# At the end of layer 1: the last pair's sum product ahead of its value products, and its transposes ahead of the preceding pair's output product

## The chip, the cores and the metric

The kernel runs on one core of one Trainium2 chip. The metric is the device time of one execution in microseconds (us); lower is better. Where two kernels are compared, the ratio is the mean time of one kernel's fast runs over that of the other's fast runs of the same rounds, so it is not quite the ratio of the medians that are quoted beside it. Intervals are 95%.

## The reference, cut to what matters

Two identical layers are applied to one token of 640 numbers. Each is an attention over a key and value cache (32 heads of 192, the last 4096 positions) and a gated MLP, each with a layer norm ahead and a residual after it:

```python
    x = A_x
    x = x + _A_ref(_layernorm(x, axis=-1), A_k_cache, A_v_cache, A_wq, A_wo)
    x = x + _B_ref(_layernorm(x, axis=-1), B_w_gate, B_w_up, B_w_down)
    x = x + _A_ref(_layernorm(x, axis=-1), A_k_cache, A_v_cache, A_wq, A_wo)
    x = x + _B_ref(_layernorm(x, axis=-1), B_w_gate, B_w_up, B_w_down)
```

With a single token every product is a matrix times a vector, so the kernel reads far more than it computes: 218 MB of keys, values and weights in some 514 us.

## The kernel before

The heads are worked on in 16 pairs, 0 to 15. For each pair there is a query product `Q`, scores `QK`, a softmax, value products `PVmm` (scores times values, followed by a copy of the result by ScalarE), a sum product `RS` (the softmax's sum, spread to all partitions, and its reciprocal on VectorE), transposes `PVt` of the copied result (and the scaling by the reciprocal on VectorE), and an output product `PVn` with that pair's part of the output weights, which adds into `yT`. The helpers record operations, and each engine executes its own in the order of recording; `ex=[rb[i]]` makes an operation wait for the other engines' last use of PSUM bank i.

```python
        def RS(z, bk=4):
            so = 260 if bk == 2 else 2 * DH
            sm = bank[bk][:, so:so + 2]
            pg.op("pe", lambda t: t.matmul(sm, lhsT=ones_f, rhs=rs2[z], start=True, stop=True), rd=[res(f"rs2{z}"), res("ones")], wr=[res("rsum")], ex=[rb[bk]])
            for h in range(2):
                rb[bk].last["dve"] = pg.op("dve", lambda v, h=h: v.reciprocal(out=Rn[z][64 * h:64 * h + 64], in_=sm[64 * h:64 * h + 64, h:h + 1]),
                                          rd=[res("rsum")], wr=[res(f"Rn{z}{h}")])
        # ... PVmm: 32 matmuls into two banks and a ScalarE copy of each bank; in the last pair the
        #     values come in two loads, three quarters (b1) and one quarter (b0), and the products that
        #     need b0 are a part of their own (24 matmuls, then 8) ...
        def PVt(z, sums=True):
            if sums:
                RS(z)
            # ... tm: six small matmuls from o8_sb into oT3, which lies in bank 2 ...
            pg.op("pe", tm, rd=[res("o8sb0"), res("o8sb1"), res("cst")], ex=[rb[2]])
            pg.op("dve", lambda v: v.tensor_scalar(out=oTb[z], in0=oT3[:, 0:3], scalar1=Rn[z], scalar2=None, op0=ALU.mult),
                  rd=[res(f"Rn{z}0"), res(f"Rn{z}1")], wr=[res(f"oTb{z}")], ex=[rb[2]])
        # ... PVn: 15 matmuls of wo and oTb[z] into yT; for pairs 14 and 15 they wait for the load "wol" ...
        if l == 0:
            # ... pairs 0 to 14 ...
            p = NPAIR - 1
            PVmm(p, 1)
            RS(1, 2)
            PVn(p - 1, 0)
            PVt(1, False)
            PVn(p, 1)
```

Then come the residual and the MLP of the layer, which begins with a mean over all partitions (`ln_mean`, one float32 matmul), a centring on VectorE, and the gate products.

All loads go through one queue, in a fixed order. SyncE issues a load when its buffer has come free. Around the end of layer 1 the order is:

```python
    def last_values(l, p):
        return [("b1", l, p), ("b0", l, p)]
    seq = [("a", 0, 0)] + [("c", 0, p) for p in range(1, 15)] + [("a", 0, 15), ("b", 0, 14)] + last_values(0, 15)
    seq += [("wol", 14), ("wol", 15)] + [(k,) for k in (*MD, "v1", "wq2", "v0", "v2", "v3", "v4", "wq3", "wom")] + # ...
```

So the values of pair 15 (`b1`, then the last quarter `b0`) are followed by the output weights of pairs 14 and 15, then by the gate weights `wg0` and `wg2` and two pieces of up weights. Those eight are issued in one go, near 258 to 262 us. The next load, `d0` (480 KB of down weights), goes into cells that held the first gate weights, so it is issued only when the first group of gate products is done. That is the first transfer that has to wait for the code that the change touches.

Of the kernel before, what the change touches and what calls it, by code (L numbers as in the profile page):

```python
# [109 lines left out]
def decode_kernel(ctx: ExitStack, nc, cx: bass.AP, uc: bass.AP,  # L110
# [66 lines left out]
    def res(name):  # L177
        if name not in R:
            R[name] = _Res(name)
        return R[name]  # L180
# [13 lines left out]
    def slot(s, o, n):  # L194
        return big[:, PLACE[s] * UNIT + o:PLACE[s] * UNIT + o + n]

    def v_at(p):
        return 0 if p % 2 else WOE
# [12 lines left out]
    def mreg(o, n):  # L211
        return big[:, M0 + o:M0 + o + n]
# [165 lines left out]
    def ln_sq(xi):  # L378
        ln_center(xi, 1, xc, res("xc"))
        pg.op("dve", lambda v: v.tensor_tensor_reduce(out=sq, in0=xc, in1=xc, scale=1.0 / D, scalar=0.0, op0=ALU.mult, op1=ALU.add,  # L380
                                                      accum_out=ss_c), rd=[res("xc")], wr=[res("sq"), res("ss")], multi=True)

    def ln_rstd(k2, eps_ap, out_ap, rout):
        pg.op("pe", lambda t: t.matmul(dmx[:, 0:1], lhsT=ones_f, rhs=ss_c, start=True, stop=True), rd=[res("ss"), res("ones")], ex=[rb[2]])
        pg.op("act", lambda a: a.activation(out=lnv_c, in_=dmx[:, 0:1], func=ACT.Ln, bias=eps_ap, scale=k2), rd=[res("eps")], wr=[res("lnv")], ex=[rb[2]])
        pg.op("act", lambda a: a.activation(out=out_ap, in_=lnv_c, func=ACT.Exp, scale=-0.5), rd=[res("lnv")], wr=[rout])
# [7 lines left out]
    def attention(l, xi):  # L394
# [6 lines left out]
        def Q(p, y, bk=2):  # L401
            qe = bank[bk][:, 0:P]
            sa = A_SLOT[l][p]
            w, rw = slot(sa, 0, WQE), [rslot[sa]]
            if (l, p) == (1, 2):
                w, rw = mreg(0, WQE), rc[0:WQE // FW]
            elif (l, p) == (1, 3):
                s2 = A_SLOT[l][2]
                w, rw = slot(s2, 0, WQE), [rslot[s2], res("wq3")]

            def f(t):
                for i, c0 in enumerate((0, P, 2 * P)):
                    for c in range(DC):
                        ins = t.matmul(qe[:, i:i + 1], lhsT=w[:, c * 2 * DH + c0:c * 2 * DH + c0 + P], rhs=xq[:, c:c + 1], start=(c == 0), stop=(c == DC - 1))  # L414
                return ins
            ev = pg.op("pe", f, rd=[res("xq")] + rw, ex=[rb[bk]])
            if y is None:
                pg.op("dve", lambda v: v.tensor_copy(out=q2, in_=qe[:, 0:3]), wr=[res("q2")], ex=[rb[bk]])
                return ev
            pg.op("dve", lambda v: v.tensor_tensor(out=qs[:, y], in0=qe[:, 0:3].unsqueeze(2).to_broadcast([P, 3, 32]), in1=mask3, op=ALU.mult),  # L420
                  rd=[res("cst")], wr=[res(f"qs{y}")], ex=[rb[bk]])
            return ev
# [49 lines left out]
# [8 lines that stand above are left out]
        def PVmm(p, z):  # L480
            inm = l == 1 and p == PM
            sv = None if inm else B_SLOT[l][p]
            half = (l, p) in halves
            for h in (1, 0) if half else (0, 1):
                vt = (mreg(h * NB * DH, NB * DH) if inm else slot(sv, v_at(p) + h * NB * DH, NB * DH)).rearrange("p (t d) -> p t d", t=NB)
                for part in (1, 0) if half and h == 0 else (None,):
                    us = range(NB // 2) if part is None else range(part * NB // 4, (part + 1) * NB // 4)
                    first = range(NB // 4, NB // 4 + 4) if part is not None else range(4)
                    final = range(NB // 4 - 4, NB // 4) if part is not None else range(NB // 2 - 4, NB // 2)

                    def f(t, h=h, vt=vt, us=us, first=first, final=final):
                        for u in us:
                            j = u % 4
                            ins = t.matmul(o8[h][32 * j:32 * j + 2, 0:2 * DH].rearrange("p (a d) -> p a d", a=2), lhsT=et_sb[:, z, h * NB + 2 * u:h * NB + 2 * u + 2],  # L494
                                           rhs=vt[:, 2 * u:2 * u + 2, :], start=u in first, stop=u in final, tile_position=(0, 32 * j))
                        return ins
                    rV = rc if inm else [rslot[sv]] + ([res("bh0")] if part == 0 else []) if half else [rval[sv]]
                    ev = pg.op("pe", f, rd=[res(f"et{z}")] + rV, ex=[rb[4 + h]])
                    if not inm and not half:
                        rslot[sv].rd.append(ev)  # L500
                pg.op("act", lambda a, h=h: a.copy(out=o8_sb[:, :, h * DH:(h + 1) * DH], in_=o8[h][:, 0:2 * DH].rearrange("p (a d) -> p a d", a=2)),  # L501
                      wr=[res(f"o8sb{h}")], ex=[rb[4 + h]])
# [5 lines left out]
# [4 lines that stand above are left out]
            def tm(t):  # L512
                for c in range(3):
                    for sg in range(2):
                        ins = t.matmul(oT3[:, c:c + 1], lhsT=o8_sb[:, sg, c:2 * DH:3], rhs=mask2[:, sg:sg + 1], start=(sg == 0), stop=(sg == 1))
                return ins
# [3 lines that stand above are left out]
# [72 lines left out]
        if l == 0:  # L592
            Q(0, 0)
            ln_sq(xi)
            QK(0, 0)
            ln_rstd(K2_ATT, eps_a, srs_c, res("srs"))
            soft(0, scale_pm)
            expo()
            ET(0)
            step(1, 0)  # L600
            loop(1, 14)
            p = NPAIR - 1
            PVmm(p, 1)
            RS(1, 2)
            PVn(p - 1, 0)
            PVt(1, False)
            PVn(p, 1)
        else:
            mark("a14_0", Q(14, 0))
            mark("QM", Q(PM, 1, 5))  # L610
            def unstow(i):
                o, n = sum(m for _, m in stash[:i]), stash[i][1]
                pg.op("dve", lambda v: words(v, mreg(o, n), stash[i][0]), rd=[res(f"stash{i}")], wr=rc[o // FW:-(-(o + n) // FW)],
                      ex=[rb[SB[i][0]]], own="st")
            for i in (3, 4, 5):
                unstow(i)
            ln_sq(xi)
            mark("a14_1", QK(14, 0, ks=(0,)))
            mark("a14_2", QK(14, 0, ks=(1, 2)))
            Q(15, 0)  # L620
            ln_rstd(K2_ATT, eps_a, srs_c, res("srs"))
            QK(15, 0, 1)
            soft(0, scale_pm)
            expo()
            ET(0)
            Q(0, 0)
            soft(1, hook=lambda: (Q(2, None), QK(0, 0)))
            for i in (2, 0, 1):
                unstow(i)
            expo(1)  # L630
            soft(0, mid=lambda: PVmm(14, 0))
            PVout(14, 0)
            ET(1)
            expo()
            PVmm(15, 1)
            ET(0)
            QK(PM, 1)
            PVout(15, 1)
            soft(0, mid=lambda: PVmm(0, 0))
            PVout(0, 0)  # L640
            expo()
            ET(1)
            pg.op("dve", lambda v: v.tensor_tensor(out=qs[:, 0], in0=q2.unsqueeze(2).to_broadcast([P, 3, 32]), in1=mask3, op=ALU.mult),
                  rd=[res("cst"), res("q2")], wr=[res("qs0")])
            packed(2, 0, PM)
            Q(3, 0)
            packed(3, 0, 2)
            loop(3, 10)
            PVmm(13, 1)
            PVout(13, 1)  # L650
# [307 lines left out]
```

## Time and profile before

| | before |
|---|---|
| time, median of the three runs | 513.91 us (513.4 to 514.08) |
| profiled span | 512.3 us |
| tensor engine busy | 260.4 us (51%) |
| load queue, share of 16 engines' span | 99.2% |
| rate over the span | 426 GB/s |

These are four lines of the page of the kernel before: the busy tenths of the DMA engines and the rate in 40 slices of the span, the one busy queue, and the engines' shares of the chain that ended last.

```profile
DMA  9999999999999999999999999999999999999996
GB/s 422 435 423 426 423 426 436 426 426 448 444 430 435 432 430 430 430 426 453 409 413 418 409 441 431 434 435 426 435 448 444 439 426 426 431 436 417 427 429 283
...
q1 hardware_dynamic: 9506, 218.14, 99.2%
...
DMA 63%; PE 24%; DVE 7%; ACT 3%; issue 2%; SPq 1%; DVEq 0%; POOL 0%; ACTq 0%; POOLq 0%
```

The transfers are busy in tenths 9 in every slice but the last, which holds the tail after the last landing. The Trainium skill (Perfetto Trace Analysis, Roofline) gives a single active core a ceiling of about 435 GB/s, set by its 16 DMA engines; 426 GB/s over the whole span is 98% of that, so this trace agrees. The transfers are also 63% of the chain that ended last.

The next view is the timeline of the kernel before at the end of layer 1, with the weight loads and some short VectorE lines left out. The columns are the start and the duration in us, engine, source line, operation, output and inputs, shapes and count, and in brackets how long the engine had been idle and what released it. L494 are value products, L475 the sum product, L501 ScalarE's copies, L529 output products, L515 the transposes, L518 the scaling, L371 the mean, L374 the centring, L684 the gate products.

```profile
268.66 1.15 PE L494 MATMUL o<-big,et_sb 128*2 128x384 bf16 x24 [0.78 <-DMA big<-in_uc_dram]
...
270.50 0.73 PE L494 MATMUL o<-big,et_sb 128*2 128x384 bf16 x8 [0.69 <-DMA big<-in_uc_dram]
...
271.15 0.59 PE L475 MATMUL bank<-sc 128*128 128x2 f32 x2
271.27 0.48 ACT L501 CAST o_sb<-o 128x384 bf16<-128x384 f32 x1 [1.26 <-PE o L494]
...
271.74 0.54 PE L529 MATMUL bank<-sh,big 128*128 128x1 bf16 x15
...
272.29 0.31 PE L515 MATMUL bank<-cst,o_sb 128*128 128x1 bf16 x6
272.63 0.22 DVE L518 TENSOR_SCALAR sh<-bank,sc 128x3 bf16<-128x3 f32 x1 [0.49 <-PE bank L515]
...
273.00 0.54 PE L529 MATMUL bank<-sh,big 128*128 128x1 bf16 x15 [0.41 <-DVE sh L518]
...
273.81 0.59 PE L371 MATMUL bank<-sc 128*128 128x1 f32 x2 [0.27 <-DVE sc L390]
274.43 0.24 DVE L374 SCALAR_TENSOR_TENSOR sh<-bank,sc 128x5 bf16<-128x5 f32 x2 [0.68 <-PE bank L371]
...
275.07 0.96 PE L684 MATMUL scores<-sh,big 128*128 128x1 bf16 x30 [0.67 <-DMA big<-in_wg_dram]
```

The value products come in two parts, each released by a landing. After them the tensor engine works without a pause to 272.6, then waits for the scaling, and pair 15's output product runs at 273.00. The centring of the MLP is done near 274.6, but the first gate product starts at 275.07, and what released it is a landing: that of the gate weights at 275.02.

The chain of waits of the kernel before, in the same region (start, duration, what):

```profile
258.26 0.33 SPq L217
...
261.49 18.52 DMA big<-in_wu_dram
...
280.06 0.84 PE scores L684 x25
...
280.91 5.59 DMA big<-in_wd_dram
```

It goes from the issue of loads at 258 to 261 us straight to a landing of up weights at 280.01 and another of down weights. Nothing of the end of layer 1 (268 to 275 us) is in it.

### The profile page before, as it was taken

What the parts mean: (1) busy time and instruction counts of PE and PEld (TensorE: products, weight loads), DVE (VectorE), ACT (ScalarE), POOL (GpSimd) and SP (SyncE); (2) the same over time, 40 slices, a digit from 0 to 9 for tenths busy, and PEclk for the clock granted to TensorE, in tenths of its full rate; (3) what the DMA queues carried; (4) which work ended last, traced back from release to release, by engine and by line L of the source; (5) the groups of instructions that cost most, each with busy time, mean ns of one, the idle gap of its engine ahead of it and who ended that gap; (6) DMA issues with size and microseconds to landing.
All of it is one profiled execution on the core that took longest, in us unless ns stands there. A gap on an engine that the chain in (4) does not pass through costs nothing.

```text
span 512.3 us, 8586 instructions
## 1 busy us (share of the span) xinstructions
PE 260.4 (51%) x3716; PEld 137.8 (27%) x3716; DVE 102.3 (20%) x386; ACT 85.2 (17%) x173; POOL 4.3 (1%) x31
## 2 busy tenths in 40 slices
PE   0452456333534464436576767775726343534655
PEld 0220222121212231223234434432312121212334
DVE  0221322112210221112121333231202112210312
ACT  1110111011101111011121023221201011101221
POOL 0010000000000000000000000000000000000000
PEclk9995655567755565666555568865665557755575
DMA  9999999999999999999999999999999999999996
GB/s 422 435 423 426 423 426 436 426 426 448 444 430 435 432 430 430 430 426 453 409 413 418 409 441 431 434 435 426 435 448 444 439 426 426 431 436 417 427 429 283
DMA packets 9670, 218.47 MB, mean 426 GB/s; under 512 B 1201, under 2 KB 1586, under 8 KB 4658
## 3 DMA queue, kind: packets, MB, share of 16 engines
q1 hardware_dynamic: 9506, 218.14, 99.2%
q8 instruction: 13, 0.21, 0.1%
q10 hardware_dynamic: 144, 0.06, 0.0%
q14 instruction: 7, 0.06, 0.0%
HBM read 218.20 MB, written 0.00 MB: 426 GB/s over the span
## 4 chain that ended last, share of the span: by engine, by line
DMA 63%; PE 24%; DVE 7%; ACT 3%; issue 2%; SPq 1%; DVEq 0%; POOL 0%; ACTq 0%; POOLq 0%
DMA big<-in_uc_dram 54%; PE scores L432 8%; PE o L494 7%; DMA big<-in_wd_dram 6%; DMA big<-in_wu_dram 4%; DVE sc L442 3%; PE bank L448 2%; PE bank L414 2%; ACT e_sb L458 2%; PE bank L529 1%; PE bank L464 1%; ACT diag L445 1%; SPq L217 1%; DVE sc L477 1%; DVE qs L420 1%
## 5 line engine op out<-in xcount | busy, mean ns | idle before, releaser
L432 PE MATMUL scores<-big,qs 128*32 128x512 bf16 x744 | 82.7, 613 | 10.3 <-DVE qs L420 9.5
L414 PE MATMUL bank<-sh,big 128*128 128x1 bf16 x465 | 17.2, 166 | 133.1 <-DMA big<-in_uc_dram 130.7
L494 PE MATMUL o<-big,et_sb 128*2 128x384 bf16 x1024 | 73.7, 453 | 7.2 <-DMA big<-in_uc_dram 4.1
L445 ACT ACTIVATE diag<-cst,sc 128x128 f32<-128x128 bf16 x32 | 12.8, 401 | 308.3 <-DVE sc L442 295.1
L442 DVE TENSOR_REDUCE sc<-scores 128x1 f32<-128x1024 f32 x31 | 37.9, 1224 | 78.3 <-PE scores L432 78.3
L414 PEld LDWEIGHTS bank<-sh,big 128*128 128x128 bf16 x465 | 14.8, 104 | 136.2 <-DMA big<-in_uc_dram 113.6
L448 PE MATMUL bank<-diag,sc 128*128 128x128 f32 x64 | 22.1, 441 | 46.6 <-ACT diag L445 46.6
L458 ACT ACTIVATE e_sb<-scores,sc 128x1024 bf16<-128x1024 f32 x31 | 37.4, 1206 | 41.6 <-DVE sc L453 39.3
L420 DVE TENSOR_TENSOR qs<-bank,cst 128x96 bf16<-128x96 f32 x30 | 7.7, 258 | 162.0 <-PE bank L414 162.0
L494 PEld LDWEIGHTS o<-big,et_sb 128*2 128x2 bf16 x1024 | 27.3, 104 | 41.2 <-issue 25.8
L432 PEld LDWEIGHTS scores<-big,qs 128*32 128x32 bf16 x744 | 24.1, 132 | 43.7 <-issue 31.2
L448 PEld LDWEIGHTS bank<-diag,sc 128*128 128x128 f32 x64 | 13.8, 269 | 72.7 <-ACT diag L445 70.5
L501 ACT CAST o_sb<-o 128x384 bf16<-128x384 f32 x64 | 29.4, 475 | 19.8 <-PE o L494 19.6
L529 PE MATMUL bank<-sh,big 128*128 128x1 bf16 x480 | 17.2, 165 | 15.4 <-DVE sh L518 15.4
L468 DVE CAST et_sb<-bank 128x64 bf16<-128x64 f32 x32 | 7.2, 225 | 68.1 <-PE bank L464 68.1
L529 PEld LDWEIGHTS bank<-sh,big 128*128 128x128 bf16 x480 | 14.6, 99 | 17.9 <-DVE sh L518 12.5
L449 DVE TENSOR_REDUCE sc<-bank 128x2 f32<-128x128 f32 x32 | 9.3, 292 | 42.8 <-PE bank L448 42.8
L464 PE MATMUL bank<-cst,e_sb 128*128 128x8 bf16 x256 | 11.7, 169 | 8.2 <-ACT e_sb L458 8.1
L464 PEld LDWEIGHTS bank<-cst,e_sb 128*128 128x128 bf16 x256 | 8.9, 101 | 24.0 <-issue 17.1
L475 PE MATMUL o<-sc 128*128 128x2 f32 x62 | 14.2, 298 | 0.6 <-ACT o_sb L501 0.6
L475 PEld LDWEIGHTS o<-sc 128*128 128x128 f32 x62 | 12.1, 244 | 2.2 <-ACT o_sb L501 1.3
L477 DVE RECIPROCAL sc<-o 64x1 f32<-64x1 f32 x62 | 10.2, 165 | 10.5 <-PE o L475 8.7
(81 smaller groups left out, 110.9 us busy)
## 6 DMA issues: line engine op xcount, KB each, us to landing
big<-in_uc_dram SPq DMA_DIRECT2D x20, 7104.0 KB, 22.7
big<-in_uc_dram SPq DMA_DIRECT2D x11, 3552.0 KB, 20.1
big<-in_uc_dram SPq DMA_DIRECT2D x2, 3072.0 KB, 17.9
big<-in_uc_dram SPq DMA_DIRECT2D x8, 480.0 KB, 6.3
big<-in_uc_dram SPq DMA_DIRECT2D x1, 2784.0 KB, 12.2
big<-in_uc_dram SPq DMA_DIRECT2D x1, 2304.0 KB, 10.3
big<-in_uc_dram SPq DMA_DIRECT2D x1, 2048.0 KB, 10.8
big<-in_wg_dram SPq DMA_DIRECT2D x2, 960.0 KB, 15.9
```

Source lines behind the costliest of these rows:

```text
L414: ins = t.matmul(qe[:, i:i + 1], lhsT=w[:, c * 2 * DH + c0:c * 2 * DH + c0 + P], rhs=xq[:, c:c + 1], start=(c == 0), stop=(c == DC - 1))
L432: ins = t.matmul(sc_x[1 + b][32 * j:32 * j + 32, :], lhsT=qs[:, y, k, :], rhs=slot(sa, WQE + k * W + (4 * b + j) * 512, 512), start=(k == ...
L442: pg.op("dve", lambda v: v.reduce_max(out=mx, in_=sc_x[0][:], axis=AX.X), wr=[res("mx")], ex=sc_x[3:5])
L445: pg.op("act", lambda a: a.mul(out=diag[:], in_=ident, mul=mx), rd=[res("cst"), res("mx")], wr=[res("diag")])
L448: pg.op("pe", lambda t: t.matmul(dmx[:, 0:P], lhsT=ones_f, rhs=diag[:], start=True, stop=True), rd=[res("diag"), res("ones")], ex=[rb[2]])
L458: pg.op("act", lambda a: a.activation(out=e_sb[:], in_=sc_x[0][:], func=ACT.Exp, bias=nbias, scale=srs_c, accum_out=rowsum), rd=[res("nbia ...
L464: ins = t.matmul(qe[:, 0:2 * NB].rearrange("p (r x) -> p r x", r=2)[:, :, 4 * b:4 * b + 4], lhsT=e_sb[:, b * P:(b + 1) * P], rhs=sel, star ...
L475: pg.op("pe", lambda t: t.matmul(sm, lhsT=ones_f, rhs=rs2[z], start=True, stop=True), rd=[res(f"rs2{z}"), res("ones")], wr=[res("rsum")], ...
L477: rb[bk].last["dve"] = pg.op("dve", lambda v, h=h: v.reciprocal(out=Rn[z][64 * h:64 * h + 64], in_=sm[64 * h:64 * h + 64, h:h + 1]), rd=[r ...
L494: ins = t.matmul(o8[h][32 * j:32 * j + 2, 0:2 * DH].rearrange("p (a d) -> p a d", a=2), lhsT=et_sb[:, z, h * NB + 2 * u:h * NB + 2 * u + 2 ...
L501: pg.op("act", lambda a, h=h: a.copy(out=o8_sb[:, :, h * DH:(h + 1) * DH], in_=o8[h][:, 0:2 * DH].rearrange("p (a d) -> p a d", a=2)), wr= ...
L529: ins = t.matmul(yT[:, j:j + 1], lhsT=wo[:, c * D + j * P:c * D + (j + 1) * P], rhs=oTb[z][:, c:c + 1], start=False, stop=(c == 2), skip_g ...
```

## The change

The intent is to shorten the chain of pair 15 after its last values have landed. The sum product does not need the values, so it can run in the time in which the tensor engine waits for them. The transposes can run as soon as ScalarE has copied, and pair 14's output product can cover the scaling on VectorE that follows them. Nothing is added or removed.

```diff
--- before.py
+++ after.py
@@ -600,10 +600,10 @@
             step(1, 0)
             loop(1, 14)
             p = NPAIR - 1
+            RS(1, 2)
             PVmm(p, 1)
-            RS(1, 2)
+            PVt(1, False)
             PVn(p - 1, 0)
-            PVt(1, False)
             PVn(p, 1)
         else:
             mark("a14_0", Q(14, 0))
```

## The prediction

> **What bounds the kernel now.** The transfers. The page gives the one busy queue 99.2% of 16 engines' span at 426 GB/s, and the slice row shows DMA at 9 in every slice but the last. By the packets' times, no pause over 0.15 us has fewer than 12 engines busy until 509.7 us. The Trainium skill (Perfetto Trace Analysis, Roofline) puts a single active core's ceiling at about 435 GB/s, from its 16 DMA engines; this trace is at 98% of that. Tensor-engine work can shorten it only by making a transfer start earlier when the queue would have run dry, or by changing the stretch after the last landing; the change does neither.
>
> **What the change does.** No work is added or removed; two moves at the end of layer 1, on the tensor engine. From the timeline at 266 to 276 us, before:
> - 268.66 value products of pair 15, first 24 (1.15 us), released by a landing; the last 8 at 270.50 (0.73), released by a landing at 270.45.
> - 271.15 sum product (0.59), 271.70 output product of pair 14 (0.54), 272.29 transposes (0.31), scaling on DVE to 272.85, output product of pair 15 at 273.00, residual 273.58, mean 273.81, centring to about 274.58.
> - 275.07 the first gate product, though its input was ready: it waits for a landing at 275.02.
>
> After: the sum product runs in the idle time before the values arrive. It shares a bank with pair 14's transposes, so it waits for DVE's read ending near 268.22: about 268.3 to 268.85. The first value products slip by about 0.2 us, which costs nothing: the last 8 wait for the landing at 270.45 anyway. They end near 271.2; the scalar engine's copy ends at 271.75, as before. The transposes start there (271.8 to 272.1), pair 14's output product covers the DVE scaling (272.1 to 272.65). Pair 15's output product is then ready at 272.65, but its weights land only at 272.74, so it starts near 272.8 instead of 273.00. So the local chain is 0.2 us shorter.
>
> **How much is on the critical path: nothing.** The next step, the first gate product, is released by the landing at 275.02 in both. The first transfer that waits for this stretch (down-projection weights, issued 275.66 when the first gate products end) joins a queue whose earlier transfers land until 280.01; their first engine is free at about 278.3. So its issue has 2.6 us of slack.
>
> **Prediction: 513.9 us** (before 513.91), range 513.2 to 514.7, which is the spread between runs. Faster by over 2%: 0.005; within 2%: 0.99; slower by over 2%: 0.005.
>
> **What would show it.** Timeline of after: the sum product ahead of the value products at about 268.3 and the idle tensor engine shorter there; transposes near 271.8, ahead of pair 14's output product; pair 15's output product 0.1 to 0.3 us earlier and now released by a landing rather than by DVE; the wait for the gate weights before the first gate product longer by the same (idle 0.67 to about 0.9); landings and issues from 275 us on where they were, to 0.1 us; DMA share and GB/s unchanged.
>
> **What would make it wrong.** A sum product held up past 270.5 would delay the values; but 2.6 us of slack lie behind. A lower transfer rate by chance: 0.2% of rate is 1 us.

## The result, and the profile after

The changed kernel took 513.72 us (median of 6 runs, 513.17 to 514.35), the kernel before 513.42 us in the same rounds (6 runs, 513.03 to 514.08). The ratio is 1.0004, interval 0.9991 to 1.0017: no difference. The result is correct. The local gain that the timelines below show, 0.19 us, would be 0.04% of the time, less than this interval can tell from zero; that it does not arrive is read from the traces, not from the times.

The same lines of the page of the kernel after:

```profile
DMA  9999999999999999999999999999999999999996
GB/s 426 430 423 426 423 431 430 426 423 448 439 439 430 440 430 426 426 430 443 418 415 415 409 444 427 434 436 427 452 439 435 430 430 426 435 435 417 432 424 281
...
q1 hardware_dynamic: 9506, 218.14, 99.2%
...
DMA 64%; PE 22%; DVE 8%; ACT 3%; issue 2%; SPq 1%; DVEq 0%; POOL 0%; ACTq 0%; POOLq 0%
```

They say the same as before: 426 GB/s, 99.2%. And its timeline at the end of layer 1 (the two output products are one merged line of 30; the weight-load line shows where the second of them starts):

```profile
267.96 0.58 PE L475 MATMUL bank<-sc 128*128 128x2 f32 x2 [0.54 <-DVE sh L518]
...
269.04 2.73 PE L494 MATMUL o<-big,et_sb 128*2 128x384 bf16 x32 [0.49 <-DMA big<-in_uc_dram]
...
271.82 0.48 ACT L501 CAST o_sb<-o 128x384 bf16<-128x384 f32 x1 [0.80 <-PE o L494]
...
272.35 0.32 PE L515 MATMUL bank<-cst,o_sb 128*128 128x1 bf16 x6 [0.58 <-ACT o_sb L501]
...
272.54 1.21 PE L529 MATMUL bank<-sh,big 128*128 128x1 bf16 x30
272.71 0.22 DVE L518 TENSOR_SCALAR sh<-bank,sc 128x3 bf16<-128x3 f32 x1 [3.77 <-PE bank L515]
273.18 0.48 PEld L529 LDWEIGHTS bank<-sh,big 128*128 128x128 bf16 x15 [0.20 <-DMA big<-in_uc_dram]
...
274.01 0.58 PE L371 MATMUL bank<-sc 128*128 128x1 f32 x2 [0.26 <-DVE sc L390]
274.63 0.24 DVE L374 SCALAR_TENSOR_TENSOR sh<-bank,sc 128x5 bf16<-128x5 f32 x2 [0.68 <-PE bank L371]
...
275.54 0.96 PE L684 MATMUL scores<-sh,big 128*128 128x1 bf16 x30 [0.94 <-DMA big<-in_wg_dram]
```

The sum product now runs at 267.96, in the gap before the values. The transposes start at 272.35, right after ScalarE's copy (271.82 plus 0.48), and the output product of pair 14 follows them. Pair 15's output product (the weight load at 273.18, its matmul at 273.19) is now released by a landing, that of its weights at 273.14, where VectorE released it before. This run's loads landed about 0.4 us later than the other's, so times are best counted from a landing: from the landing of pair 15's last values to the start of its output product it is 2.36 us (270.83 to 273.19), where it was 2.55 (270.45 to 273.00). That is a local gain of 0.19 us. It ends at the gate products: the tensor engine's idle time before them has grown from 0.67 to 0.94 us, and they still start 0.05 us after the landing of the gate weights, in both kernels.

The chain of waits of the kernel after, in the same region:

```profile
258.21 0.54 PE bank L529 x15
...
262.13 18.34 DMA big<-in_wu_dram
...
281.37 5.45 DMA big<-in_wd_dram
```

As before it passes from issues near 262 us to landings near 280 and 287 us, over the heads of all the moved instructions.

### The profile page after: what moved, and what is told of

Same layout as the page of the kernel before. It is cut to its first block, busy times and chain, and to the rows that moved or that the text cites. A ratio compares the mean times of both kernels' runs of the same rounds, so it can differ in the third digit from the quotient of the medians.

```text
span 512.6 us, 8586 instructions
## 1 busy us (share of the span) xinstructions
PE 255.9 (50%) x3716; PEld 135.9 (27%) x3716; DVE 102.2 (20%) x386; ACT 84.9 (17%) x173; POOL 4.2 (1%) x31
## 3 DMA queue, kind: packets, MB, share of 16 engines
q1 hardware_dynamic: 9506, 218.14, 99.2%
## 4 chain that ended last, share of the span: by engine, by line
DMA 64%; PE 22%; DVE 8%; ACT 3%; issue 2%; SPq 1%; DVEq 0%; POOL 0%; ACTq 0%; POOLq 0%
DMA big<-in_uc_dram 54%; PE scores L432 8%; DMA big<-in_wd_dram 6%; PE o L494 6%; DMA big<-in_wu_dram 4%; DVE sc L442 3%; PE bank L448 2%; ACT e_sb L458 2%; PE bank L414 2%; PE bank L529 1%; PE bank L464 1%; SPq L217 1%; ACT diag L445 1%; DVE sc L477 1%; DVE qs L420 1%
## 5 line engine op out<-in xcount | busy, mean ns | idle before, releaser
L494 PE MATMUL o<-big,et_sb 128*2 128x384 bf16 x1024 | 70.8, 440 | 6.3 <-DMA big<-in_uc_dram 2.1
L477 DVE RECIPROCAL sc<-o 64x1 f32<-64x1 f32 x62 | 10.2, 165 | 9.5 <-PE o L475 7.7
```

The source lines that it names most:

```text
L494: ins = t.matmul(o8[h][32 * j:32 * j + 2, 0:2 * DH].rearrange("p (a d) -> p a d", a=2), lhsT=et_sb[:, z, h * NB + 2 * u:h * NB + 2 * u + 2 ...
```

## The experiments

Three theories stand against each other. **Theory Q:** the queue of transfers sets the time, and the end of layer 1 has slack (it could come later by some time at no cost), so that a shorter chain only makes a longer wait. **Rival A:** the chain is on the critical path, but a gain of one half of the change was eaten by a loss of the other. **Rival B:** the gain is real but hidden by the late landing of pair 15's output weights. The numbers "from the values" below count from the landing of the last values (all 16 engines) to the start of pair 15's output product. The traces of e1 to e4 that are on file are of a second execution of these kernels; what is read below is of the first, and where the second bears on it, it is named.

### One half at a time (e1, e2)

```diff
 # e1
+            RS(1, 2)
             PVmm(p, 1)
-            RS(1, 2)
             PVn(p - 1, 0)
 # e2
+            PVt(1, False)
             PVn(p - 1, 0)
-            PVt(1, False)
```

> Only the sum product moves ahead of the value products; the transposes stay behind pair 14's output product. Theory Q (the transfer queue sets the time, the stretch has slack): ratio to before 0.998 to 1.002. Locally the first value products wait for the sum product's end (0 to 0.3 us after their landing); pair 14's output product follows the value products directly (about 271.2), the transposes start at the end of the scalar engine's copy, and pair 15's output product starts within 0.15 us of its weights' landing: this half alone already has the whole local gain. Rival A (the stretch is on the critical path and a gain of one half was eaten by a loss of the other): this half alone departs from 1 by more than 0.1%, opposite to the other half.

Measured for e1: 513.57 us against 513.41, ratio 1.001 (0.9993 to 1.0027). From the values 2.40 us, and pair 15's output product starts 0.11 us after its weights' landing, as expected: this half alone has nearly the whole local gain. One detail was wrong. Pair 14's output product did not follow the value products directly; it started at 271.56, 0.13 us after the landing of its own weights at 271.43. I had not looked at that landing. So the transposes behind it came at 271.96, 0.30 us after ScalarE's copy and not at its end. (In the second trace: 2.38, 0.10 and 0.13 us.)

> Only the transposes move ahead of pair 14's output product; the sum product stays behind the value products. Theory Q: ratio 0.998 to 1.002; locally the sum product runs while the scalar engine copies, the transposes start at the copy's end, pair 14's output product covers the scaling, and pair 15's output product again starts within 0.15 us of its weights' landing, so this half alone has the whole local gain too. Rival A: as told for the other half, departs from 1 by over 0.1%, in the other direction.

Measured for e2: 513.42 us against 513.41, ratio 1.0009 (0.9992 to 1.0026). Locally my expectation failed: from the values 2.63 us (2.62 in the second trace), which is no gain over the 2.55 of before. The lines of its timeline show why:

```profile
270.99 0.59 PE L475 MATMUL bank<-sc 128*128 128x2 f32 x2
271.11 0.48 ACT L501 CAST o_sb<-o 128x384 bf16<-128x384 f32 x1 [1.34 <-PE o L494]
...
272.12 0.30 PE L515 MATMUL bank<-cst,o_sb 128*128 128x1 bf16 x6 [0.55 <-DVE sc L477]
```

ScalarE's copy ends at 271.59, but the transposes start at 272.12, released by L477, which is VectorE's reciprocal of the sum product. Sum product and transposes share bank 2, and the bookkeeping makes the transposes wait for the reciprocals that read that bank. With the sum product behind the value products, that wait outlasts the copy. So the two halves are not interchangeable: the moved sum product is what opens the way for the transposes. Neither half departs from the kernel before in time beyond its interval, and both read on the same side of 1, so rival A's picture of a gain and a loss of over 0.1% that cancel has no support. Parts as small as the local gain (0.04%) these times could not show.

### A delay put into the chain (e3, e9, e10, e4)

If the chain has slack, a delay must cost nothing up to some size and then cost time. In the changed kernel the mean's product at the start of layer 1's MLP was repeated; the result stays correct.

```diff
-    def ln_mean():
-        pg.op("pe", lambda t: t.matmul(qe[:, 0:1], lhsT=ones_f, rhs=rs_c, start=True, stop=True), ...
+    def ln_mean(reps=1):
+        def f(t):
+            for _ in range(reps):
+                ins = t.matmul(qe[:, 0:1], lhsT=ones_f, rhs=rs_c, start=True, stop=True)
+            return ins
+        pg.op("pe", f, ...
-        ln_mean()
+        ln_mean(1 if last else N)      # N = 3, 6, 9, 17
```

> The changed kernel with the mean's product of the first layer's MLP done 3 times (same result): the chain after the residual is about 1.0 to 1.2 us longer (one took 0.59). Theory Q: the first gate product starts 0.4 to 0.8 us after its weights' landing instead of 0.05, the first transfer that waits for it is issued as much later, the queue doesn't run dry, the time stays: ratio 0.998 to 1.002. Rival A (chain on the critical path): 1.0 to 1.2 us longer, ratio about 1.002 to 1.0023, with the landings after 282 us later by that.

> As the one before, 17 times: the chain is about 8 to 9.4 us longer. Theory Q: the slack is about 0.4 us of waiting for the gate weights plus at most 2.6 us until the queue runs dry, less about 1.3 us from an issue to its first data; so the queue falls idle and the time grows by 5 to 7.5 us (ratio 1.010 to 1.015), less than the delay. In the trace a pause of the transfers of that length near 280 us. Rival A: grows by the whole delay, 8 to 9.4 us (1.016 to 1.018). Rival C (slack far larger than read): under 2 us.

The expectation of e4 already takes the time from an issue to its first data off the slack, which leaves about 1.7 us instead of 3.05. (It is put at 1.3 us; in e10 and in the second trace of e4 12 engines were busy 1.29 and 1.25 us after the issue of `d0`.) After the runs with a starved queue (e5 to e8, told further below) the size was corrected once more (theory Q2), and two more doses were run to test it:

> The changed kernel with the mean's product 6 times, a delay of 1.1 to 2.0 us (the trace will say which). Theory Q2, corrected by the four runs with a starved queue: from issue to the first engine's landing, a transfer of 480 KB that finds the queue empty took 2.8 to 2.9 us, against 3.78 in the kernel before, so the issue has 0.9 us of slack, with 0.45 of waiting for the gate weights 1.35 in all. The first landing of the first down-projection piece follows that of the transfer ahead of it by 1.17 us plus what the delay exceeds 1.35: 1.1 to 1.9 us. Time ratio 0.9985 to 1.002. The slack of my prediction, 2.6 plus 0.45: nothing lost, spacing 1.17.

> The same, 9 times, a delay of 2.3 to 3.5 us. Theory Q2: spacing 1.17 plus delay less 1.35, so 2.1 to 3.3 us; time longer by 0.9 to 2.1 us, ratio 1.0015 to 1.0045. The slack of my prediction (3.05 in all): spacing under 1.6, time longer by under 0.4 us, ratio under 1.001.

The delay is the time of the repeated product in the trace less the 0.58 to 0.59 us of a single one. It was put into the changed kernel, so that kernel's own row is the one to compare with. "Spacing" is from the first engine's landing of the last load queued ahead (up weights) to that of `d0`.

| run | repeats | delay, us | gate products after their weights' landing, us | `d0`: issue to first landing, us | spacing, us | ratio of times |
|---|---|---|---|---|---|---|
| before | 1 | 0 | 0.05 | 3.78 | 1.17 | 1 |
| after | 1 | 0 | 0.05 | 3.40 | 1.17 | 1.0004 (0.9991 to 1.0017) |
| e3 | 3 | 0.24 | 0.05 | 3.78 | 1.23 | 1.0011 (0.9994 to 1.0027) |
| e3, second trace | 3 | 0.86 | 0.32 | 3.52 | 1.53 | as above |
| e9 | 6 | 0.91 | 0.40 | 3.42 | 1.19 | 1.0006 (0.9994 to 1.0017) |
| e10 | 9 | 3.42 | 2.93 | 2.77 | 2.82 | 1.0051 (1.0038 to 1.0064) |
| e4 | 17 | 6.82 | 6.34 | 2.85 | 6.54 | 1.0107 (1.0088 to 1.0126) |
| e4, second trace | 17 | 6.14 | 5.57 | 2.90 | 5.93 | as above |

e10's spacing and e4's time are in the ranges stated, e10's time (1.0015 to 1.0045 stated) is above its range; e9 is as stated, but its delay came out below both sizes of the slack, so it does not tell them apart. Medians: e3 514.12, e4 519.1 (before in those rounds 513.41), e9 513.27, e10 516.15 (before 513.5).

Three of the four delays were outside what I had stated. In e3 and e9 the tensor engine's granted clock during the repeated products was 1.00, and in e9 12 matmul instructions took 1.50 us; in e10 and e4 it was 0.50, as for the single product of before, and in e10 18 took 4.00. In the second trace of e3 it was 0.50 as well, and its six took 1.44 us instead of 0.83. The Trainium skill (TensorE: Matmul & The Clock Gate, Part 1) says that the clock is halved by default and released after sustained activity, with a window that runs free of the kernel; the clocks of 1.00 and 0.50 in these traces agree with the halving, and the window itself no run here shows. The clock does not explain e4: there each further product added 0.43 us (7.41 less 0.59, over 16) at the same clock at which a single one takes 0.59. The wrong delays make e3 a weak test, and e9 only bounds the slack from below. e10 and e4 answer the question.

A delay of 0.91 us cost nothing that the runs can see, and the spacing stayed at 1.19. The delays of 3.42 and 6.82 us moved the spacing by 1.65 (2.82 less 1.17) and 5.37 us, so 1.8 and 1.45 us of them were absorbed. That is the slack: about 1.4 to 1.8 us (1.4 in e4's second trace). It has two parts. The wait for the gate weights took up about 0.53 us of either delay (the delay less the growth of the fourth column, as from 0.05 to 2.93). And `d0` took 3.78 us from its issue to its first landing behind other loads in the kernel before, but only 2.77 to 2.93 us when it found the queue empty (e10, e4 and, below, e5 to e8), so its issue could be 0.9 to 1.0 us later. These sizes hold to some 0.4 us: the kernel after, with no delay, has 3.40 where before has 3.78, and in e3's second trace the spacing grew by 0.36 us at a delay of 0.86, while e9 with 0.91 lost nothing.

The windows of the stretch around that point, of the kernel before, and below it of e10. The columns are named in the first line; the last three are granted clock, DMA share and GB/s.

```profile
core 0: us, PE busy (x) PEld busy (x) DVE busy (x) ACT busy (x) POOL busy (x), PEclk, DMA share, GB/s
276.00:278.00 2.00, 0.67 (x26) 0.64 (x25) 0.00 (x0) 0.00 (x0) 0.00 (x0) 0.50 1.03 426
278.00:280.00 2.00, 1.01 (x25) 0.93 (x21) 0.35 (x2) 0.73 (x3) 0.00 (x0) 0.50 1.02 419
280.00:282.00 2.00, 1.36 (x40) 1.23 (x40) 0.28 (x2) 0.00 (x0) 0.00 (x0) 0.50 1.01 387
282.00:284.00 2.00, 0.74 (x22) 0.66 (x23) 0.00 (x0) 0.00 (x0) 0.00 (x0) 0.50 1.02 411
```

```profile
276.00:278.00 2.00, 1.65 (x25) 1.60 (x25) 0.54 (x6) 0.00 (x0) 0.00 (x0) 0.50 0.98 405
278.00:280.00 2.00, 2.00 (x68) 2.00 (x64) 0.00 (x0) 0.26 (x1) 0.00 (x0) 0.50 0.60 160
280.00:282.00 2.00, 0.76 (x29) 0.67 (x26) 0.63 (x3) 0.47 (x2) 0.00 (x0) 0.50 0.77 234
282.00:284.00 2.00, 0.42 (x15) 0.34 (x13) 0.00 (x0) 0.00 (x0) 0.00 (x0) 0.50 0.95 362
```

In e10 the rate falls from 405 to 160 and 234 GB/s while the queue restarts, where the kernel before holds 387 to 426. In e4 the chain of waits, which passed over the end of layer 1 before, now runs through the repeated product (7.42 us from 273.33) and the issue of `d0` at 281.65. The time lost can be read from the GB/s column; the DMA share (0.60, 0.77) shows less of it, since the engines count as busy while they move little.

More was lost than the spacing shows. Time grew by 2.6 us in e10 (0.0051 of 513.5), against 1.65 in the spacing, so counted in time only 0.8 us of its delay was free, and 1.3 us of e4's (6.82 less 0.0107 of 513.4). In e10 the second load, `d1`, landed 1.98 us after `d0` on the first engine, where that distance is 1.17 in the kernel before, and its issue took 1.60 us on SyncE instead of 0.41 (2.22 and 1.58 in e4). This is not shown to be a cost of the empty queue: in e4's second trace and in e5 to e8, where `d0` found the queue empty too, `d1` was issued in 0.40 to 0.41 us and landed 1.18 to 1.30 us after it, and an issue of 1.2 us is found without any delay as well (1.17 at 289.38 in the kernel before, 1.26 in e1's second trace). What makes single issues long was not found out.

### The load order (e5, e6)

To see the change without the wait for pair 15's output weights, the last load of the values (`b0`, a quarter of them; the expectation calls it a half) was put behind both of them, in the kernel before (e5) and in the changed one (e6). Bytes and result are the same.

```diff
-    seq = ... + [("a", 0, 15), ("b", 0, 14)] + last_values(0, 15)
-    seq += [("wol", 14), ("wol", 15)] + ...
+    seq = ... + [("a", 0, 15), ("b", 0, 14)] + [("b1", 0, 15), ("wol", 14), ("wol", 15), ("b0", 0, 15)]
+    seq += ...
```

> Old order of products, but the last half of pair 15's values is loaded behind the output weights of pairs 14 and 15 instead of ahead of them (same bytes, same result), so the values land last, near 272.7, and nothing but the products follows them. Theory Q: the last value products start at about 272.8, then sum product, pair 14's output product, transposes, scaling and pair 15's output product one after the other, about 2.5 us from the last value product's start to pair 15's output product; the first gate product comes 2.0 to 2.5 us after its weights' landing, and the transfers issued after it 2.0 to 2.4 us later than before. The slack is about used up (under 1 us of pause), time ratio 0.999 to 1.003. Rival B (the gain is hidden only because pair 15's weights land late; with that out of the way the new order shows in the time): this run is slower by 2 us (1.004) and the one with the new order is not.

> The same load order with the new order of products. Theory Q: from the last value products' start to pair 15's output product about 2.1 to 2.3 us, so 0.2 to 0.5 us shorter than with the old order: that is the most this change can be worth anywhere, since the scalar engine's copy stands between the value products and the transposes in both. Time ratio 0.999 to 1.003, no difference to the old order beyond the noise. Rival B: faster than the old order under this load order by over 0.15%.

The timelines of e5 (old order), and below it of e6 (new order), from the last value products on:

```profile
272.69 0.81 PE L494 MATMUL o<-big,et_sb 128*2 128x384 bf16 x8 [2.02 <-DMA big<-in_uc_dram]
...
273.43 0.59 PE L475 MATMUL bank<-sc 128*128 128x2 f32 x2
...
273.88 0.54 PE L529 MATMUL bank<-sh,big 128*128 128x1 bf16 x15
...
274.57 0.30 PE L515 MATMUL bank<-cst,o_sb 128*128 128x1 bf16 x6
...
275.27 0.54 PE L529 MATMUL bank<-sh,big 128*128 128x1 bf16 x15 [0.41 <-DVE sh L518]
...
277.01 1.74 PE L684 MATMUL scores<-sh,big 128*128 128x1 bf16 x60 [0.35 <-DVE sc L374]
```

```profile
272.38 0.81 PE L494 MATMUL o<-big,et_sb 128*2 128x384 bf16 x8 [2.97 <-DMA big<-in_uc_dram]
273.24 0.48 ACT L501 CAST o_sb<-o 128x384 bf16<-128x384 f32 x1 [3.62 <-PE o L494]
...
273.77 0.32 PE L515 MATMUL bank<-cst,o_sb 128*128 128x1 bf16 x6 [0.59 <-ACT o_sb L501]
...
273.95 1.08 PE L529 MATMUL bank<-sh,big 128*128 128x1 bf16 x30
...
276.24 1.74 PE L684 MATMUL scores<-sh,big 128*128 128x1 bf16 x60 [0.35 <-DVE sc L374]
```

Old order: 2.62 us from the values' landing (272.65) to pair 15's output product (275.27). New order: 2.17 us (272.33 to 274.50). The local gain is now 0.45 us, in the range stated, and the gate products start 2.09 us after their weights' landing in e5 and 1.62 in e6; `d0` was issued at 277.58 in e5, 1.9 us later than before, and landed 2.36 us after the load ahead of it on the first engine instead of 1.17: a pause of 1.2 us, where under 1 was stated. In time: 514.64 us (e5) and 514.61 (e6), before 513.49; ratios 1.0017 (1.0000 to 1.0034) and 1.0014 (0.9997 to 1.0031). Rival B expected 2 us between the two, and 0.15% at the least; 0.03 us is seen. It falls at that size. A remainder stays open: with the slack used up, as here, 0.45 us in the chain ought to be worth up to 0.45 us of time, which is 0.09% and below what these intervals can resolve. The traces, one of each, point that way: with the new order `d0` landed 1.59 us after the load ahead of it instead of 2.36 on the first engine, and 1.79 instead of 2.08 on the mean of the 16.

### Fewer bytes, in three places (e7, e8, e11, e12)

If the bytes set the time, 983 thousand bytes fewer should bring 2.3 us at 426 GB/s. e7 (old order) and e8 (new order) leave out the output weights of pairs 14 and 15; e11 loads only half of the second MLP's gate weights; e12 shortens one of layer 2's large loads in the middle of its loop. Their outputs are wrong, which doesn't matter for the times. The comparison with the reference rejected e11 (relative error 0.256); it passed e7, e8 and e12, whose stale data moved the output by less than its tolerance.

```diff
 # e7, e8
-    seq += [("wol", 14), ("wol", 15)] + [(k,) for k in ...
+    seq += [(k,) for k in ...
 # e11
-            pg.dma(q_dma(mreg(0, 12 * FW), wg_d), "fg", wr=rc)
+            pg.dma(q_dma(mreg(0, 6 * FW), wg_d[:, 0:6 * FW]), "fg", wr=rc)
 # e12
-            pg.dma(q_dma(slot(first, 0, 2 * UNIT), uc[p]), ...
+            n = 2 * UNIT - (3840 if (l, p) == (1, 9) else 0)
+            pg.dma(q_dma(slot(first, 0, n), uc[p][:, 0:n]), ...
```

> Old order, and the output weights of pairs 14 and 15 (983 KB) are not loaded at all (the result is wrong on purpose). Theory Q: the time falls by those bytes at the measured rate, 983 KB at 426 GB/s = 2.3 us, ratio 0.9945 to 0.9968, although no work of any engine is taken away: the gate weights land about 2.3 us earlier, and now the centring and not the landing releases the first gate product. Rival A (chain on the critical path): the chain from the values' landing on is unchanged, so under 0.5 us.

> New order without those weights (wrong on purpose). Theory Q: the same fall of about 2.3 us (0.9945 to 0.9968), and no difference to the old order without them beyond 0.1%; locally pair 15's output product no longer waits for weights and starts 0.2 to 0.5 us earlier, counted from the values' landing, than in the old order, and so does the first gate product. Rival A: the local gain appears in the time.

> The kernel before, with only half of the second MLP's gate weights loaded (960 KB, 983 thousand bytes, fewer; wrong result on purpose), at a place where two transfers and more are queued ahead. Theory Q2: here nothing that is issued later depends on a chain, so the whole of 983 KB at 426 GB/s = 2.3 us comes off: ratio 0.9945 to 0.9965, where the same bytes taken from the end of layer 1 brought only 1.0 to 1.3 us because the chain took over there. Rival (bytes are not what sets the time): under 0.5 us.

> The kernel before, with one of layer 2's large loads (pair 9's keys) shorter by 3840 columns of 128 rows, 983 KB (wrong result on purpose), in the middle of the steady loop, where a whole further load of 16.7 us is queued behind it and the products of a pair end some 6 us before their buffers are needed again. Theory Q2: no chain can take over here, and everything up to the end comes earlier: landings after it by 2.3 us, and the time too, ratio 0.9945 to 0.9965, where the same bytes at the end of layer 1 brought 1.0 to 1.3 us and at the end of the kernel 1.4. Rival (bytes set the time only loosely everywhere): about 1.0 to 1.4 us here as well, ratio 0.997 to 0.998.

| run | where | this, us | before, us | ratio |
|---|---|---|---|---|
| e7 | end of layer 1, old order | 512.69 | 513.49 | 0.998 (0.9962 to 0.9998) |
| e8 | end of layer 1, new order | 512.44 | 513.49 | 0.9975 (0.9951 to 0.9998) |
| e11 | end of the kernel | 512.18 | 513.5 | 0.9973 (0.996 to 0.9985) |
| e12 | steady loop of layer 2 | 511.65 | 513.32 | 0.9958 (0.9944 to 0.9971) |

Only e12 brought the bytes' worth: 0.0042 of 513.3 is 2.2 us. The other three missed what I expected of them. In e7 and e8 the gate weights did land about 2.3 us earlier (in e7 2.28 us after the last values' landing, against 4.57 in the kernel before), but the chain did not move with them: the gate products came 2.02 us (e7) and 1.56 us (e8) after the landing, now released by the centring, and `d0` was issued too late for a queue that had emptied sooner. From e7's times: the gate products started 4.31 us after the values' landing instead of 4.62, 0.3 us earlier, and the slack of the issue adds 0.9 to 1.0; the sum, about 1.25 us, is an estimate of the gain, and 1.0 us was measured. The same sum for e8 (3.84 instead of 4.62) is 1.7 us, and 1.3 was measured; the intervals, some 1 us to either side, hold both. In e11 the landings behind the shortened load did come 2.3 us earlier in the trace, but the last MLP's products follow the end of its attention and not a landing: its gate products started at 500.41 us against 500.46, its up products at 505.26 against 505.32, and the end waited for them.

So bytes set the time where no chain can take over within the bytes' worth; at the end of layer 1 the chain took over after the 1.0 to 1.3 us that were measured. In e7 and e8 it had taken over, and there the new order's chain was 0.46 us shorter (from the values 2.54 and 2.08 us). The times, 1.0 and 1.3 us below the kernel before, differ in the right direction, but far inside their intervals, so it is not shown that the change is worth anything there.

## Why the prediction was right

- **What bounds the kernel.** Right: the transfers do. e12 shows it from the other side, with 2.2 us for 983 thousand bytes, and e4 and e10 show that the time grows when the queue runs dry.
- **The local chain.** Right in its parts and its sum. The sum product went into the gap, the transposes to the end of ScalarE's copy, pair 15's output product to its weights' landing; 0.2 us was predicted, and 0.19 us measured. One step did not happen: I had the value products slip by 0.2 us behind the sum product. In the run after, the sum product was over at 268.54 and the values landed at 269.00. One reading of the prediction is off, and nothing rests on it: by the packets' times fewer than 12 engines are busy from about 508 us on, not from 509.7.
- **Nothing of it on the critical path.** Right: the wait before the gate products grew (0.67 to 0.94 us idle, 0.9 predicted), and they started 0.05 us after their weights' landing in both kernels.
- **"Landings and issues from 275 us on where they were, to 0.1 us".** Wrong as put. On the first engine the landing of the gate weights moved by 0.08 us, but on the last engine, which the products wait for, by 0.47, and the issue of `d0` by 0.46. The change is not the cause: the landing near 113 us, long before the changed code, was already 0.84 us later (113.04 and 113.88), and e1, e2 and e3 have the gate weights' landing at -0.17, -0.22 and +0.12 (-0.17, 0.00 and +0.32 in the second traces). One should compare intervals from a landing, not times from the start.
- **"Its issue has 2.6 us of slack".** This is the step that failed, though the outcome did not depend on it. I took the time from the issue to when the first engine is free of the queue's earlier loads, and left out the latency of a load that finds the queue empty. It took 2.77 to 2.93 us from issue to first landing there, against 3.78 behind others, so the slack of the issue is 0.9 to 1.0 us. With the wait ahead of the gate products the whole is 1.4 to 1.8 us by the delays, and 0.8 to 1.3 counted in time, not the 3.05 (2.6 and 0.45) that I had read. A chain 2 us longer runs into this, as e5's did; for a shorter one any slack will do. The Trainium skill (DMA: Bandwidth & Descriptors, Anatomy of one DMA) gives a fixed cost of about 2.0 us plus the bytes at 436 GB/s, fitted for another issue path; for `d0`'s 491,520 bytes that is an estimate of 3.1 us. It is between the 2.8 us on the first engine and the 3.7 us on the last one of e10, so to read that section would have given the size of the term that I left out.

## What to carry to other kernels

When one resource is busy without a pause, ask of a shortened chain which transfer is issued earlier because of it, and whether the queue would have been empty by then. If neither, the gain becomes a longer wait in front of the next landing, however real it is in the timeline. Measure such slack with a delay of growing size rather than read it off two timestamps, and count the latency of a load into an empty queue against it; here it was about half of what the timestamps suggested, or less.

## What the Trainium skill lacked or had wrong

- DMA: Bandwidth & Descriptors (Anatomy of one DMA) fits a fixed cost for loads issued from GpSimd only. For a load of 480 KB issued from SyncE into an empty queue these runs show 2.77 to 2.93 us from the issue to the first engine's landing, and to the last one's 3.7 to 4.1 us, once 5.91 (e4 to e8, e10).
- No page says what a queue that ran dry costs beyond the pause. In e10 the time grew by 2.6 us where the spacing grew by 1.65; the cause of the rest stays open.
- DMA: Bandwidth & Descriptors warns that the 16 engines of a load finish independently, but gives no size in time. Here the first and the last engine's landing of one large load lay 1.50 us apart near 113 us in one run and 2.31 in another of nearly the same program, and it moved the waits at the end of layer 1 by some 0.4 us.
